# Identity and mask made on the chip, the first weight pieces fetched apart, and four steps moved in the order of a recurrent attention and feed-forward kernel

## The chip, the cores and the metric

The kernel runs on one core of a Trainium2 chip. The core has a matrix engine (TensorE, PE in the profile), a vector engine (VectorE, DVE), a scalar engine (ScalarE, ACT), a general one (GpSimd, POOL) and an engine that issues most of the transfers (SyncE, SP). Each runs its own instruction queue in order and waits for the others through semaphores. TensorE writes into PSUM, a small memory of eight banks that VectorE and ScalarE read; everything else lies in SBUF, 128 partitions wide.

The metric is the device time of one execution in microseconds (us). Before the change the median of 8 runs is 381.15 us, with 380.92 the lowest and 381.96 the highest.

## The reference

The first half is a gated linear attention, a recurrence over 768 tokens for 4 batches and 8 heads of width 48; the second is a feed-forward block with a softmax-weighted activation and a layer norm.

```python
# attention: q, k, v, alpha are (4, 8, 768, 48), float32
for t in range(S):
    state = alpha[:, :, t, :, None] * state + np.einsum('bhd,bhe->bhde', k[:, :, t], v[:, :, t])
    y[:, :, t] = np.einsum('bhd,bhde->bhe', q[:, :, t], state)

# feed-forward on x = y as (3072 tokens, 384); w_in (384, 1024), w_out (1024, 384)
h = x @ w_in
e = np.exp(h - np.max(h, axis=-1, keepdims=True))
solu = h * e / (np.sum(e, axis=-1, keepdims=True) + 1e-09)
mu = np.mean(solu, axis=-1, keepdims=True)
var = np.mean((solu - mu) ** 2, axis=-1, keepdims=True)
return ((solu - mu) / np.sqrt(var + 1e-06) * g_ln) @ w_out
```

The two weight matrices arrive as 64-bit floats and are turned into 32-bit ones on the chip.

## The kernel before

The 768 tokens are cut into six groups of 128. A group holds 128 tokens of each of the four batches, 512 in all, and passes two phases. In the attention phase the recurrence is replaced by products within the group: alpha, keys and queries are turned so that the head width lies on the partitions (32 partitions for each batch; the 48 of a head are split into a block of 32 and, two heads together, one of 32, twelve blocks in all). Running products of alpha (`scan_back`, `scan_on`, both the scan of L222) scale keys (L243) and queries (L254); TensorE forms scores (L281), which are masked to the lower triangle (L292) and multiplied with the values (L315) beside a product with the state carried from earlier groups; `next_state` (L364, L374) carries the state on. In the up phase the 1024 hidden columns are taken in eight tiles f of 128: `up_mm` (L389) multiplies, `up_act` forms the exponential on ScalarE (L403), the product h times e on VectorE (L404) and its square on ScalarE (L405); `running` (L420) adds up squares on VectorE and exponentials on GpSimd. `down` (L500) multiplies by the second weights, chunk by chunk of 128 tokens; `finish` (to L541) forms the norm from the sums (L523, L525, L528 on VectorE, L537 on GpSimd), for the first group adds the mean's part (L533), scales on ScalarE (L539) and writes out.

All order is written out by hand; nothing is scheduled automatically. Four PSUM banks `a0` to `a3` serve attention, two `h` the up phase, two `o` the down phase.

**The start.** SP issues the first loads in this order: alpha, k, q, v (two transfers each, rows of 48 floats), and the first four of eight weight pieces with `fetch` (L569). ACT's queue loads the 128x128 identity, the mask (ones on and above the diagonal), a parity table and the gains. GpSimd clears buffers: `vt`, `unit`, `aT`, `hT`, `seed`, `state`. VectorE sets constants, `ones` first among them. TensorE then runs 16 matmuls on `ones` alone to warm up and turns alpha, k and q by matmuls with the identity (L171).

`fetch(i, slot, n)` brings n pieces beginning with piece i into the slots of 1536 floats of `room` that begin at `slot`. A piece of w_in is 256 of its columns in 64 bits, over three blocks of 128 rows; `fetch(0, 3, 2)` brings pieces 0 and 1 with three transfers of 512 KB whose rows hold both. `bits(i, part)` turns a piece into 32-bit floats in five VectorE operations: part 0 is L599 and L602, part 1 is L607, L610 and L611; without a part both are done. `in_range(i)` tests a piece's size on ScalarE (L586, L587).

**The first group.** After the scores of both halves of the heads, VectorE masks batches 0 and 1 of the first half (`masked(0, range(2))`), while ScalarE copies batches 2 and 3 out and GpSimd masks them (L712, L713). VectorE then masks all four batches of the second half (`masked(1)`) and converts piece 0 (`bits(0)`). `read_values(0)` on TensorE takes batch after batch; each needs heads of both halves. Behind it on TensorE stand the turning of the gains and of the keys (`keys_back`, L300, copied out by ScalarE in L302) and the first up tile, which needs piece 0 converted.

**The turn to the second up phase.** While group 0's output and group 1's attention end, group 2's alpha and keys are prepared: three backward scans, the turning of the keys (L197, L200), their product on GpSimd (L243, two operations), and `scan_on(2, 2)`, the forward scan of the third block of four. Then come `read_values(1)`, a test of alpha on ScalarE (L214) and the last part of chunk 3's `down`, with `finish(3)` at the end. The loop over up phases g = 1 to 5 follows; in step s of eight it runs up tile s, then what the plan names under `behind`: for g = 1 in step 0 the state and the v load, in step 1 the forward scans of blocks 0 and 1 (`on0 on1`), in step 2 the turning of the queries' last 16 (`lasts`, L200, followed by GpSimd's product with `qe`) and of their first 32 (`firsts`, L197, followed by two products with `qv`), in step 3 `apart` (L247). `running` comes after `behind`; `after` names the chunk whose `finish` runs behind the next up tile.

Of the kernel before, what the change touches and what calls it, by code (L numbers as in the profile page):

```python
# [14 lines left out]
ALU = mybir.AluOpType  # L15
AX = mybir.AxisListType
P = 128
# [15 lines left out]
def fast_path(ctx, tc, q, k, v, alpha, moe_w_in, moe_w_out, moe_g_ln, out):  # L33
# [12 lines left out]
    nc = tc.nc  # L46
    B, H, S, D = q.shape
# [30 lines left out]
    ident = const.tile([P, P], FP, name="ident")  # L78
    mask = const.tile([P, P], FP, name="mask")
    ones = const.tile([P, P], FP, name="ones")  # L80
# [148 lines left out]
    def scan_on(g, i):  # L229
        part = slice(NP * i, NP * i + NP)  # L230
        if i == 2:

            nc.vector.reciprocal(out=seed[:, :, 0:1], in_=h4[:, :, 1:2])
            nc.scalar.copy(out=fend[:, g], in_=h4[:, :, 1])
        scan(aT[:, part], aT[:, part], seed[:, part], False)
# [53 lines left out]
    def masked(half, batches=range(B)):  # L289
        a = masks[half]  # L290
        for b in batches:
            nc.vector.tensor_tensor(  # L292
                out=sT[:, b, half * NP : half * NP + NP], in0=a[b], in1=mask[:, None, :].to_broadcast([P, NP, P]),
                op=ALU.mult,
            )
# [47 lines left out]
    def read_values(g, batches=range(B)):  # L343
        if 0 in batches:
            gr[g]["x"] = pair.tile([P, KC, B, P], FP, name="x")
        for b in batches:
            for n, part in enumerate(parts):
                for a, r, h, e in part:
                    y_mm(b, a, r, 0, vn[:, b, h, e], sT[:, b, h], n == len(parts) - 1)
        for b in batches:  # L350
            nc.scalar.copy(out=gr[g]["x"][:, :, b], in_=reading["y"][b])
# [159 lines left out]
    def finish(n):  # L511
        g, b = divmod(n, B)
        d = st[n]
        s, o = sums[:, n], d["o"][:, 0:DM]
        t0 = b * S + g * P
        if g == G - 1:
            o_sb = work.tile([P, DM], FP, name="o_sb")
            r = gr[g]["r"][:, b : b + 1]
            nc.scalar.activation(out=o_sb, in_=o, func=AF.Copy, scale=r)
            nc.scalar.dma_start(out=out[t0 : t0 + P, :], in_=o_sb)  # L520
            d.clear()
            return
        nc.vector.tensor_copy(out=s[:, 0:1], in_=d["o"][:, DM : DM + 1])  # L523
        t = small.tile([P, 1], FP, name="t")
        nc.vector.scalar_tensor_tensor(  # L525
            out=t, in0=s[:, 0:1], scalar=-1.0 / DFF, in1=s[:, 0:1], op0=ALU.mult, op1=ALU.mult
        )
        nc.vector.tensor_tensor(out=s[:, 3:4], in0=t, in1=gr[g]["s"][:, b : b + 1], op=ALU.add)  # L528
        if g == 0:

            if not d.get("moved"):
                o = work.tile([P, DM + 1], FP, name="o_mean")[:, 0:DM]
            nc.vector.scalar_tensor_tensor(  # L533
                out=o, in0=mean_sb, scalar=s[:, 0:1], in1=d["o"][:, 0:DM], op0=ALU.mult, op1=ALU.add
            )
        r = small.tile([P, 1], FP, name="r")
        nc.gpsimd.tensor_tensor(out=r, in0=s[:, 3:4], in1=mhalf, op=ALU.pow)  # L537
        o_sb = work.tile([P, DM], FP, name="o_sb")
        nc.scalar.activation(out=o_sb, in_=o, func=AF.Copy, scale=r)  # L539
        nc.sync.dma_start(out=out[t0 : t0 + P, :], in_=o_sb)  # L540
        d.clear()  # L541
# [16 lines left out]
    def fetch(i, slot, n=1):  # L558

        kind, f = pieces[i]  # L560
        w = n * F // (2 if kind else KC)
        raw = room[:, 1536 * slot : 1536 * (slot + n)].bitcast(U32).rearrange("p (c f w) -> p c f w", f=w, w=2)
        if kind:
            parts = [(slice(0, P), c, moe_w_out[(f + c) * P : (f + c + 1) * P, :]) for c in range(2)]
        else:
            parts = [(slice(0, P), c, moe_w_in[c * P : (c + 1) * P, f * P : f * P + w]) for c in range(KC)]
        for rows, c, src in parts:
            if float64:
                nc.sync.dma_start(out=raw[rows, c].rearrange("p f w -> p (f w)"), in_=src.bitcast(U32))  # L569
            else:  # L570
                dst = w_out[rows, f + c, 0:DM] if kind else w_in[rows, c, f * P : f * P + w]
                nc.sync.dma_start(out=dst, in_=src)
        for m in range(n):
            raws[i + m] = raw[:, :, w // n * m : w // n * (m + 1)]
# [14 lines left out]
    def bits(i, part=None):  # L589
        if not float64:  # L590
            return
        lo, hi = raws[i][:, :, :, 0], raws[i][:, :, :, 1]
        if part != 1:
            made[i] = [
                two.tile([P, F], FP, tag="two", name=x).rearrange("p (c f) -> p c f", c=hi.shape[1])
                for x in ("top", "low")
            ]
            top = made[i][0].bitcast(U32)
            nc.vector.tensor_scalar(  # L599
                out=top, in0=hi, scalar1=3, scalar2=0x3FFFFFF8, op0=ALU.logical_shift_left, op1=ALU.bitwise_and  # L600
            )
            nc.vector.scalar_tensor_tensor(  # L602
                out=top, in0=hi, scalar=0xC0000000, in1=top, op0=ALU.bitwise_and, op1=ALU.bitwise_or
            )
        if part != 0:
            top, low = made.pop(i)
            nc.vector.tensor_scalar(  # L607
                out=low.bitcast(U32), in0=top.bitcast(U32), scalar1=0xFF800000, scalar2=None, op0=ALU.bitwise_and
            )
            nc.vector.scalar_tensor_tensor(out=low, in0=lo, scalar=2.0**-52, in1=low, op0=ALU.mult, op1=ALU.mult)  # L610
            nc.vector.tensor_tensor(out=place(i), in0=low, in1=top, op=ALU.add)  # L611
# [34 lines left out]
    def inline(x, name):  # L646
        return nc.inline_tensor(np.ascontiguousarray(x, np.float32), name=name).ap()

    load_first(alpha, an, 0)
    nc.scalar.dma_start(out=ident, in_=inline(np.eye(P), "ident_c"))  # L650
    nc.scalar.dma_start(out=mask, in_=inline(np.triu(np.ones((P, P))), "mask_c"))
    odd = np.arange(P) // E1 % 2
    nc.scalar.dma_start(out=parity, in_=inline(np.stack([1 - odd, odd], 1), "parity_c"))
    nc.scalar.dma_start(out=g_rows, in_=moe_g_ln.rearrange("(c p) -> c p", p=P))
# [7 lines left out]
    nc.gpsimd.memset(seed, 0.0)  # L662
    nc.gpsimd.memset(state, 0.0)
    load_v_first(0)
    fetch(0, 3, 2)
    fetch(2, 1, 2)
    nc.vector.memset(ones, 1.0)
    nc.vector.memset(small_ones, 1.0 / 32)
    nc.vector.memset(mhalf, -0.5)
    nc.vector.memset(mone, -1.0)  # L670
# [26 lines left out]
    for i in (2, 0, 1):  # L697
        if i == 1:
# [3 lines left out]
            out=qe if i == 2 else qv[:, part], in0=t[i], in1=aT[:, part, 1:SW], op=ALU.mult  # L702
# [7 lines left out]
    for b in (2, 3):  # L710
        s = sT[:, b, 0:NP]
        nc.scalar.copy(out=s, in_=masks[0][b])  # L712
        nc.gpsimd.tensor_tensor(out=s, in0=s, in1=mask[:, None, :].to_broadcast([P, NP, P]), op=ALU.mult)  # L713
    masked(0, range(2))
    masked(1)
    bits(0)
    read_values(0)
    gains()
    keys_back(0)
# [94 lines left out]
    for i in range(3):  # L814
# [2 lines left out]
    keys(2)  # L817
    load(k, kn, 3)
    scan_on(2, 2)
    read_values(1)  # L820
    alpha_over(2)
    load(alpha, an, 3)
    down(3, 1, slice(3, HF))
    finish(3)

# [2 lines left out]
        behind={0: "states v keys", 1: "load on2 on0 on1", 2: "lasts firsts", 3: "apart", 5: "decay", 6: "alpha", 7: "back"},  # L830
# [2 lines left out]
    )  # L833
    first = dict(
        head={3: "keys_back", 5: "masked0", 6: "masked1"},
        behind={0: "states v", 1: "on0 on1", 2: "lasts firsts", 3: "apart", 5: "decay", 7: "alpha back"},
        tail={4: "scores0", 5: "scores1", 6: "begin read0 read1"},
        middle={7: "read2 read3 values"},
    )
# [51 lines left out]
    for g in range(1, G + 1):  # L891
        rise, att = g < G, g + 1 < G
        plan = first if g == 1 else usual

        def at(where, s):
            for what in plan[where].get(s, "").split() if att else ():
                attend(g + 1, what)

        after = None
        if not rise:  # L900
            break
        for s in range(FC):
            at("head", s)
            if rise:
                up(g, s)
            if after is not None:
                finish(after)
                after = None
            if s == 0 and g > 1:
                token_sums(g - 1)  # L910
            at("behind", s)
            for f in centres.get(s, ()) if g == 1 else ():
                centre(f)
            if rise and s:
                running(g, s)
            at("middle", s)
            if rise and s == FC - 1:
                todo.append((g * B, 0))
            step = todo.pop(0)
            if step:  # L920
                n, half = step
                down(n, half)
                if half:
                    after = n
            at("tail", s)
        if after is not None:
            finish(after)
        todo = [(n, half) for n in range(g * B, g * B + B) for half in range(2)][1:]
# [492 lines left out]
```

## Time and profile before

| what | us |
| --- | --- |
| median of 8 runs | 381.15 |
| the profiled execution | 380.4 |
| its span | 378.6 |
| TensorE busy, of the span | 365.6 (97%) |
| VectorE busy | 244.1 (64%) |
| ScalarE busy | 146.9 (39%) |
| GpSimd busy | 128.4 (34%) |
| TensorE's granted clock, mean | 0.997 |

The span runs from the first instruction to the end of the last one; the rest of the profiled execution's time lies around it. A matmul's end is modelled, so TensorE's busy share says little of how much it could still take. In a timeline row the first number is the start in us, the second the length of the row, then engine, line of the kernel, operation, what is written and read (partitions x elements), how many equal instructions the row joins, and in brackets how long the engine was idle before and what ended that. "issue" names a wait that the profile can't put down to anything.

### The profile page before, as it was taken

Reading aid. Unit: us, or ns where it says so; the run is one execution under the profiler, and the core shown is the slowest. Engines: PE = TensorE matmul, PEld = TensorE weight load, DVE = VectorE, ACT = ScalarE, POOL = GpSimd, SP = SyncE. Lnnn points to the kernel's source line nnn. Section 1 sums busy time; section 2 is a strip of 40 time slices with the busy share of each in tenths; the row PEclk is TensorE's granted clock in tenths of the full one; section 3 lists DMA queues with packets and bytes.
Section 4 is the critical chain, followed back from the end, with each engine's and each line's share of the span. In section 5 each row is a group of like instructions: output and inputs, shape, how many; then the busy total and the mean of one; then the engine's idle time right before and its main releaser. Section 6 shows DMA issues by size and latency. Waiting matters only on the chain.

```text
span 378.6 us, 10523 instructions
## 1 busy us (share of the span) xinstructions
PE 365.6 (97%) x4659; PEld 219.4 (58%) x4659; DVE 244.1 (64%) x379; ACT 146.9 (39%) x263; POOL 128.4 (34%) x134
## 2 busy tenths in 40 slices
PE   8789999999898999999999999999999999999995
PEld 8675355566654565555675555675556675555552
DVE  1988889979988876874665875665865411455410
ACT  3638874593445152224451224451233131233110
POOL 5040000042246970662630671630672420333210
PEclk9999999999999999999999999999999999999998
DMA  9984999304096001950002940002300000000011
GB/s 187 193 307 119 222 273 141 85 2 126 26 226 128 4 5 34 197 126 21 23 25 41 205 111 23 23 24 46 61 0 23 24 23 2 22 21 21 23 46 48
DMA packets 65526, 30.78 MB, mean 81 GB/s; under 512 B 47032, under 2 KB 63680, under 8 KB 65472
## 3 DMA queue, kind: packets, MB, share of 16 engines
q1 hardware_dynamic: 64448, 29.10, 34.5%
q10 hardware_dynamic: 1024, 0.92, 0.7%
q8 instruction: 38, 0.62, 0.7%
q14 instruction: 16, 0.13, 0.1%
HBM read 25.30 MB, written 4.72 MB: 79 GB/s over the span
## 4 chain that ended last, share of the span: by engine, by line
PE 72%; DVE 14%; ACT 5%; issue 3%; DMA 3%; SPq 2%; POOL 0%; ACTq 0%; DVEq 0%
PE o L500 30%; PE h L389 24%; PE y L315 8%; PE a L281 5%; SPq L153 2%; DVE hT L222 2%; DVE room L404 2%; DMA qn<-in_q_dram 2%; DVE sT L292 1%; ACT sq L586 1%; DMA out_dram<-o_sb 1%; DVE aT L197 1%; PE kv L364 1%; PE tp L300 1%; DVE top L602 1%
## 5 line engine op out<-in xcount | busy, mean ns | idle before, releaser
L500 PE MATMUL o<-w_out,room 128*128 128x385 f32 x384 | 133.8, 491 | 0.0
L389 PE MATMUL h<-x,w_in 128*128 128x512 f32 x288 | 132.5, 599 | 0.6 <-DVE room L404 0.3
L500 PEld LDWEIGHTS o<-w_out,room 128*128 128x128 f32 x384 | 71.2, 190 | 55.8 <-issue 13.1
L389 PEld LDWEIGHTS h<-x,w_in 128*128 128x128 f32 x288 | 52.8, 189 | 59.8 <-issue 47.9
L404 DVE TENSOR_TENSOR room<-h,e 128x512 f32<-128x512 f32 x40 | 27.6, 689 | 82.0 <-ACT e L403 81.9
L403 ACT ACTIVATE e<-h 128x512 f32<-128x512 f32 x40 | 23.9, 598 | 107.5 <-PE h L389 107.5
L420 POOL TENSOR_TENSOR p<-p,e 128x512 f32<-128x512 f32 x30 | 41.8, 1394 | 15.7 <-ACT e L403 15.6
L537 POOL TENSOR_TENSOR r<-sums,mhalf 128x1 f32<-128x1 f32 x20 | 14.9, 745 | 78.6 <-DVE sums L528 78.5
L405 ACT ACTIVATE u<-room 128x512 f32<-128x512 f32 x40 | 25.2, 631 | 36.9 <-DVE room L404 36.9
L292 DVE TENSOR_TENSOR sT<-a,mask 128x512 f32<-128x512 f32 x42 | 26.1, 682 | 8.3 <-PE a L281 8.2
L263 POOL TENSOR_TENSOR state<-state,hT 128x192 f32<-128x192 f32 x20 | 11.2, 580 | 52.8 <-DVE hT L222 52.8
L243 POOL TENSOR_TENSOR kT<-kT,hT 128x1024 f32<-128x1024 f32 (+1 forms) x8 | 14.2, 1798 | 42.2 <-DVE kT L197 42.2
L222 DVE TENSOR_TENSOR_SCAN hT<-aT,unit 128x516 f32<-128x516 f32 x18 | 23.1, 1347 | 7.6 <-ACT aT L683 7.5
L420 DVE TENSOR_TENSOR p<-p,u 128x512 f32<-128x512 f32 x30 | 23.0, 768 | 6.5 <-ACT u L405 6.5
L281 PEld LDWEIGHTS a<-qv,kT 32*128 32x128 f32 x704 | 21.9, 186 | 8.7 <-issue 2.4
L281 PE MATMUL a<-qv,kT 32*128 32x128 f32 x704 | 24.7, 278 | 1.9 <-POOL qv L254 1.1
L222 DVE TENSOR_TENSOR_SCAN aT<-aT,seed 128x516 f32<-128x516 f32 x18 | 26.3, 1494 | 0.2
L315 PE MATMUL y<-sT,vn 128*32 128x128 f32 x768 | 23.6, 274 | 2.2 <-issue 1.7
L315 PEld LDWEIGHTS y<-sT,vn 128*32 128x32 f32 x768 | 20.9, 110 | 4.4 <-issue 3.4
L214 ACT ACTIVATE sq<-an,mone 128x1536 uint8<-128x1536 f32 x12 | 18.9, 1574 | 0.2
L315 PE MATMUL y<-qv,state 32*32 32x128 f32 x960 | 16.6, 277 | 0.0
L539 ACT ACTIVATE o_sb<-o,r 128x384 f32<-128x384 f32 x16 | 9.3, 581 | 18.8 <-POOL r L537 18.8
(146 smaller groups left out, 371.9 us busy)
## 6 DMA issues: line engine op xcount, KB each, us to landing
an<-in_alpha_dram SPq DMA_DIRECT2D x20, 192.0 KB, 4.5
vn<-in_v_dram SPq DMA_DIRECT2D x10, 384.0 KB, 6.3
out_dram<-o_sb SPq DMA_DIRECT2D x20, 192.0 KB, 1.9
room<-in_moe_w_in_dram SPq DMA_DIRECT2D x6, 512.0 KB, 8.1
room<-in_moe_w_out_dram SPq DMA_DIRECT2D x8, 384.0 KB, 4.3
kn<-in_k_dram SPq DMA_DIRECT2D x16, 192.0 KB, 4.5
qn<-in_q_dram SPq DMA_DIRECT2D x16, 192.0 KB, 3.7
kn<-in_k_dram SPq DMA_DIRECT2D x4, 384.0 KB, 5.8
```

Of the source, the lines that this page charges most:

```text
L214: nc.scalar.activation(out=sq, in_=x, func=AF.Relu, scale=sign, bias=mone, accum_out=over[:, g, i : i + 1])
L222: nc.vector.tensor_tensor_scan(out=o, data0=a, data1=s, initial=1.0, op0=ALU.mult, op1=ALU.add)
L281: nc.tensor.matmul(a[b][:, i], lhsT=kT[quarter(b), kb], rhs=qv[quarter(b), qb], start=kb == h, stop=kb != h, tile_position=(32 * b, 0), sk ...
L292: nc.vector.tensor_tensor(out=sT[:, b, half * NP : half * NP + NP], in0=a[b], in1=mask[:, None, :].to_broadcast([P, NP, P]), op=ALU.mult,)
L315: nc.tensor.matmul(y_bank(b)[quarter(r), a], lhsT=lhsT, rhs=rhs, start=(b, r) not in begun, stop=stop, tile_position=(row, 32 * r), skip_g ...
L389: nc.tensor.matmul(h, lhsT=w_in[:, a, f * P : (f + 1) * P], rhs=d["x"][:, a].rearrange("p b t -> p (b t)"), start=(a == 0), stop=(a == KC ...
L403: nc.scalar.activation(out=e, in_=h, func=AF.Exp)
L404: nc.vector.tensor_tensor(out=u, in0=h, in1=e, op=ALU.mult)
L405: nc.scalar.activation(out=u2, in_=u, func=AF.Square)
L420: eng.tensor_tensor(out=p, in0=d[0][i] if f == 1 else p, in1=d[f][i], op=ALU.add)
L500: nc.tensor.matmul(d["o"][:, 0 : DM + 1], lhsT=u_of(g, f)[:, b * P : b * P + P], rhs=w_out[:, f], start=(f == 0), stop=(f == FC - 1), skip ...
L537: nc.gpsimd.tensor_tensor(out=r, in0=s[:, 3:4], in1=mhalf, op=ALU.pow)
```

## The change

- The loads of the identity and the mask on ACT's queue go. VectorE's setting of `ones` moves up, and GpSimd makes both matrices from it with two `affine_select` operations at the head of its queue, before it clears buffers.
- Pieces 0 and 1 are fetched by two calls instead of one: six transfers of 256 KB instead of three of 512 KB, and each piece lies in a slot of its own, with its 768 numbers of 64 bits in one run.
- Part 0 of `bits(0)` stands between `masked(0, range(2))` and `masked(1)`, part 1 behind `masked(1)`.
- `finish(3)` moves from before the loop to step 0 of g = 1, behind the first up tile and ahead of the state.
- The forward scan of block 0 of group 2 moves from step 1 to before `read_values(1)`, directly behind that of block 2.
- `lasts` moves from step 2 to step 1, ahead of the forward scan of block 1.

```diff
     load_first(alpha, an, 0)
-    nc.scalar.dma_start(out=ident, in_=inline(np.eye(P), "ident_c"))
-    nc.scalar.dma_start(out=mask, in_=inline(np.triu(np.ones((P, P))), "mask_c"))
+    nc.vector.memset(ones, 1.0)
+    for x, op in ((ident, ALU.is_equal), (mask, ALU.is_ge)):
+        nc.gpsimd.affine_select(
+            out=x, in_=ones, pattern=[[1, P]], compare_op=op, fill=0.0, base=0, channel_multiplier=-1
+        )
...
     load_v_first(0)
-    fetch(0, 3, 2)
+    fetch(0, 3)
+    fetch(1, 4)
     fetch(2, 1, 2)
-    nc.vector.memset(ones, 1.0)
...
     masked(0, range(2))
+    bits(0, 0)
     masked(1)
-    bits(0)
+    bits(0, 1)
     read_values(0)
...
     scan_on(2, 2)
+    scan_on(2, 0)
     read_values(1)
     alpha_over(2)
     load(alpha, an, 3)
     down(3, 1, slice(3, HF))
-    finish(3)
...
     first = dict(
...
-        behind={0: "states v", 1: "on0 on1", 2: "lasts firsts", 3: "apart", 5: "decay", 7: "alpha back"},
+        behind={0: "states v", 1: "lasts on1", 2: "firsts", 3: "apart", 5: "decay", 7: "alpha back"},
...
-        after = None
+        after = B - 1 if g == 1 else None
```

## The prediction

> **What bounds the kernel now.** I read the page's busy shares and its chain first, then the chain in order of time, then the timelines of the two stretches that the change touches.
>
> ```profile
> PE   8789999999898999999999999999999999999995
> PE 72%; DVE 14%; ACT 5%; issue 3%; DMA 3%; SPq 2%; POOL 0%; ACTq 0%; DVEq 0%
> ```
>
> From about 129 us on, the chain is PE alone without a hole, so time won or lost there can't be made up: whatever shift exists at 129 us reaches the end. Before that the chain changes hands, and these pieces of it say who sets the first up phase:
>
> ```profile
> 24.55 3.04 PE y L315 x101
> ...
> 28.36 0.90 ACT kg L302 x2
> ...
> 29.92 0.90 ACT sq L586 x2
> ...
> 31.82 1.04 ACT sq L586 x2
> ...
> 33.81 0.49 ACT sT L403
> ```
>
> The y matmuls of read_values end at 27.59; then ScalarE works without a gap (kg copies, two range tests) up to the first exponential. ScalarE, not DVE, holds the pace until 56.49 us; DVE waits before almost every L404. So this stretch is as late as y's end, and DVE work finished earlier gains nothing in it. From 57 to 105 us DVE runs back to back.
>
> The stretch of the masks:
>
> ```profile
> 20.18 1.29 DVE L292 TENSOR_TENSOR sT<-a,mask 128x512 f32<-128x512 f32 x2 [0.30 <-PE a L281]
> 22.01 1.29 DVE L292 TENSOR_TENSOR sT<-a_h,mask 128x512 f32<-128x512 f32 x2 [0.55 <-PE a_o L281]
> 24.82 0.95 DVE L599 TENSOR_SCALAR top<-room 128x768 uint32<-128x768 uint32 x1 [0.32 <-DMA room<-in_moe_w_in_dram]
> 25.80 0.96 DVE L602 SCALAR_TENSOR_TENSOR top<-room,top 128x768 uint32<-128x768 uint32 x1
> ...
> 48.34 0.55 DVE L599 TENSOR_SCALAR top<-room 128x768 uint32<-128x768 uint32 x1
> ```
>
> ```profile
> 20.93 2.51 POOL L713 TENSOR_TENSOR sT<-sT,mask 128x512 f32<-128x512 f32 x2 [0.20 <-ACT sT L712]
> ```
>
> ```profile
> 22.75 1.07 PE L315 MATMUL y<-sT,vn 128*32 128x128 f32 x23 [0.42 <-DVE sT L292]
> 24.55 3.04 PE L315 MATMUL y<-sT,vn 128*32 128x128 f32 x101 [0.72 <-issue]
> ```
>
> DVE idles 0.55 + 0.32 = 0.87 us around the masks. PE resumes y at 22.75, when the first mask of the second half is done (22.01 + 0.69), and has one hole of 0.72.
>
> The turn of the stages, DVE and GpSimd:
>
> ```profile
> 103.04 2.40 DVE L222 TENSOR_TENSOR_SCAN aT<-aT,seed 128x516 f32<-128x516 f32 x1
> 105.52 0.91 DVE L525 SCALAR_TENSOR_TENSOR t<-sums 128x1 f32<-128x1 f32 x1
> 108.42 0.69 DVE L404 TENSOR_TENSOR room<-h,e 128x512 f32<-128x512 f32 x1 [1.27 <-ACT e L403]
> 110.90 2.96 DVE L222 TENSOR_TENSOR_SCAN aT<-aT,seed 128x516 f32<-128x516 f32 x2
> 115.94 2.05 DVE L197 STREAM_TRANSPOSE qv<-qn 128x1024 f32<-128x1024 f32 x1
> ```
>
> ```profile
> 102.17 4.24 POOL L243 TENSOR_TENSOR kT<-kT,hT 128x1024 f32<-128x1024 f32 x2 [8.29 <-DVE kT L197]
> 110.33 1.30 POOL L420 TENSOR_TENSOR p<-e 128x512 f32<-128x512 f32 x1 [3.08 <-ACT e L403]
> 116.22 1.18 POOL L254 TENSOR_TENSOR qe<-qe,aT 128x512 f32<-128x512 f32 x1 [4.59 <-DVE qe L200]
> ```
>
> The reader is to see how one engine holds up the other. A scan takes 1.2 us (two in 2.4), but 2.40 beside the key product; a 128x1 operation usually of 0.16 takes 0.91 and ends with the key product (102.17 + 4.24 = 106.41). Each waits until the GpSimd product that runs is over, and a GpSimd product that comes meanwhile waits in turn. Transposes (one input) are not held: 2.05 beside qe. L292 and L404, with one input in PSUM, aren't either.
>
> **The start.** Two loads of 64 KB leave ACT's queue. By bytes, 131 KB at the page's 187 to 193 GB/s is 0.69 us; by rows, alpha, k and q are 12,288 rows landing in about 12.7 us, so 256 rows are 0.26, part of them sent before alpha. I take 0.2 us (0 to 0.69): alpha's scan at 8.61 and q's transposes at 14.66 both move, so masked(0) ends at 21.27 instead of 21.47. The two GpSimd selections have no row. Bounds: a quarter of the 0.53 memset (0.1) to a whole 512 product (1.3) each. PE's warming covers the identity until 6.46; `unit`, ready at 3.17, becomes ready by 6.1 at worst and is read after 8.4; so they cost nothing unless the pair takes over 4.9 us. Moving `ones` up moves nothing behind it.
> [...]
>
> **The fetch.** Three issues become six, each about 0.44 us on SP; pieces 2 and 3, then 1.3 us later in issue, land near 28.5 and are read at 35, which covers that. Piece 0 is half of the 1.57 MB that landed at 24.8; at 307 GB/s (page, third slice) it lands 2.6 us earlier, near 22.0 after the 0.2; at the earliest soon after v, whose copy starts at 19.13. An early landing changes nothing, since DVE asks for it at 21.24. Fetched alone its rows are contiguous, as piece 4's are, so L599 falls from 0.95 to 0.55 (those are its bounds).
>
> **Half a conversion between the masks.** L599 wants to start at 21.24, inside the first GpSimd mask (20.73 to 22.0 after the shift; the second to 23.24). Is it held? It has one input, like the transposes, but at 768 words in 0.55 us it reads 1.4 words/ns, like the two-input p<-u,u (1024 in 0.66: 1.55), not like a transpose (1024 in 2.05: 0.5). I count it as held: 22.0 to 22.47. Then the second GpSimd mask, waiting, runs to 23.65, and L602, with two inputs, waits for it and ends at 24.5. A landing after 22.0 puts L599 behind the second mask instead and ends at 24.7. masked(1) is queued behind L602, and PE's y waits for it: first mask done at 24.45 + 0.69 = 25.14, against 22.70. PE then needs 28 + 96 = 124 records at 27.6 ns (2.76/100) plus 0.28: y ends at 25.19 + 3.42 + 0.28 = 28.9 instead of 27.6, since 0.72 of hole goes away. **+1.3 us**, the start's gain included. Other ends: L599 at 0.95 and not held, L602 behind the second mask, done at 24.1: +0.9. L599 at 0.55 and not held, L602 asking at 21.8, before the second mask: -0.3; with 0.69 at the start, -0.8. Hole not gone: +2.0. The half conversion left over ends at 29.5, before PE has finished the key transposes at 30.5: hidden.
> [...]
>
> **The turn.** finish(3) goes behind the first L404, scan_on(2,0) in front, the qe transpose (1.1 us) before scan_on(2,1). GpSimd's queue now has qe's product ahead of its first p. ScalarE is free at 105.0, so the exponential e ends at 105.6 and the 1.27 us hole goes. Then: first scan done 105.44; the second is held by the key product to 106.43, done 107.55; L404 to 108.2; finish 108.1 to 109.15 (now unheld); state sums to 110.2. But o_sb (L539, 0.62) stands before the next exponential on ScalarE, r on GpSimd (0.55) before it: that exponential ends at 110.4, against 110.26, so the second L404 gains nothing: 111.1. qe's transpose to 112.1; scan_on(2,1) 112.0 to 113.2; qe's product, held, 113.2 to 114.35; p<-u,u behind it to 114.95 (this wait of 1.15 is new); third L404 114.9 to 115.6, against 115.04. Only one transpose is left after it, but ScalarE sets the fourth: square 116.2, three kg copies (1.54) 117.7, exponential 118.2, L404 at 118.25 against 118.45. apart, scores and masks follow: **-0.2 us**. Unheld, the third L404 would come at 113.8 and the fourth at 117.4 (ScalarE) or earlier: -1.1. A late r: +0.3. SP's order of the out write and the v load stays; v, issued at 108.72, goes 2 us later and is read at 137.
>
> **Sum.** +1.3 - 0.2 = +1.1 us on a profiled execution of 380.4 (span 378.6 and 1.8 around it), so 381.5 there; the median of 8 runs stands 0.75 above it at 381.15: **382.2 us**. A measurement here tells 0.2%, 0.76 us, from no change.
>
> **Rivals.**
> - Two-way cancelling: L599 isn't held and stays near +0.9, and the turn gives 0.2 to 1.1. +0.9 - 0.6 = +0.3: 381.4, no change. For it: one input; the hole of 1.27 is real. Against: two holds are shown at the turn's places. 30%.
> - [...] 14%.
> - [...] 6%.
>
> The forecast has 50%, and 381.6 to 382.9 of its own. Range 380.6 to 383.1: up to y's hole staying (+0.7), down through the cancelling case with the turn at its best. Faster 0.14, same 0.31, slower 0.55.
>
> **What would show it.** Right: L602 between the masks at over 1.5 us, PE's y ending near 28.9, the first exponential (L403) near 35.0; no 1.27 hole at the turn, but a p<-u,u of about 1.8 there; the scores (L281) of the second up phase begin within 0.5 us of 119.6 plus the shift. Wrong: L602 at 0.96 in place, y ending by 27.6, or the fourth L404 over 0.8 us earlier against y's end.

## The result and the profile after

| | before | changed |
| --- | --- | --- |
| median | 381.24 us (31 runs) | 382.76 us (11 runs) |
| lowest to highest | 380.55 to 382.64 | 382.06 to 383.32 |
| profiled execution, its span | 380.4, 378.6 | 383.03, 381.3 |
| ratio of the runs, 95% interval | | 1.0036 (1.0026 to 1.0047) |

The changed kernel is slower by about 1.4 us. The page of the changed kernel, with the rows that answer to those of before (40 slices of 9.5 us; then the chain that ended last):

```profile
PE   8869999999998999999999999999999999999995
...
PEclk9989999999999999999999999999999999999999
...
PE 70%; DVE 12%; ACT 7%; SPq 4%; issue 3%; DMA 2%; ACTq 0%; DVEq 0%
```

From the fourth slice on nothing has changed in kind. What is new stands in the third slice (19 to 28.6 us): TensorE is busy for 6 tenths of it instead of 8, and its granted clock is 8 tenths. The rows of VectorE, GpSimd and TensorE there, from the timeline (start, length, engine, line, operation):

```profile
20.52 1.29 DVE L292 TENSOR_TENSOR sT<-a,mask 128x512 f32<-128x512 f32 x2 [0.30 <-PE a L281]
22.23 0.73 DVE L599 TENSOR_SCALAR top<-room 128x768 uint32<-128x768 uint32 x1 [0.42 <-DMA room<-in_moe_w_in_dram]
22.99 1.90 DVE L602 SCALAR_TENSOR_TENSOR top<-room,top 128x768 uint32<-128x768 uint32 x1
24.82 1.28 DVE L292 TENSOR_TENSOR sT<-a_h,mask 128x512 f32<-128x512 f32 x2
...
31.27 0.56 DVE L599 TENSOR_SCALAR top<-room 128x768 uint32<-128x768 uint32 x1
```

```profile
21.27 2.81 POOL L716 TENSOR_TENSOR sT<-sT,mask 128x512 f32<-128x512 f32 x2 [0.47 <-ACT sT L715]
```

```profile
22.27 0.41 PE L315 MATMUL y<-sT,vn 128*32 128x128 f32 x4
25.55 5.35 PE L315 MATMUL y<-sT,vn 128*32 128x128 f32 x124 [2.87 <-DVE sT L292]
```

L602, 0.96 us elsewhere, takes 1.90: it ends 0.81 us, nearly its own time, after the GpSimd masks (L713 before, L716 now; 21.27 + 2.81 = 24.08). So masked(1) begins at 24.82 instead of 22.01, and TensorE has a hole of 2.87 us. That much was forecast. The y matmuls behind the hole were not: 124 records take 5.35 us, where the rate of before would give 3.7. The windows view says why (stretch, length, busy time and number of each engine, granted clock, share of the DMA engines, GB/s):

```profile
22.00:24.00 2.00, 0.68 (x17) 0.29 (x12) 1.74 (x2) 0.00 (x0) 2.00 (x2) 1.00 0.89 197
24.00:26.00 2.00, 0.45 (x16) 0.45 (x18) 2.00 (x3) 0.00 (x0) 0.14 (x2) 1.00 0.99 331
26.60:30.00 3.40, 3.40 (x76) 3.27 (x67) 3.07 (x5) 0.97 (x3) 0.00 (x0) 0.50 0.52 211
30.00:32.00 2.00, 2.00 (x38) 1.78 (x31) 0.86 (x3) 1.27 (x3) 0.00 (x0) 0.99 0.00 0
```

In the last column but two stands TensorE's clock: 1.00, then 0.50 for the 3.4 us from 26.6 to 30.0, then full again. Half speed for 3.41 us (26.63 to 30.04 in the trace) costs 1.7 us of matmul time. The first exponential of the up phase, before and in the changed kernel:

```profile
33.72 0.58 ACT L403 ACTIVATE sT<-h 128x512 f32<-128x512 f32 x1
```

```profile
37.05 0.58 ACT L403 ACTIVATE sT<-h 128x512 f32<-128x512 f32 x1
```

It comes 3.33 later, and nearly all of the lateness is carried to the turn (3.22 at 94 us, 3.1 to 3.2 at 103).

The turn gives back 0.8 of it (2.38 from 126 us on). Its rows on VectorE and GpSimd:

```profile
108.47 2.15 DVE L222 TENSOR_TENSOR_SCAN aT<-aT,seed 128x516 f32<-128x516 f32 x1
110.54 0.66 DVE L404 TENSOR_TENSOR room<-h,e 128x512 f32<-128x512 f32 x1
...
113.45 0.69 DVE L404 TENSOR_TENSOR room<-h,e 128x512 f32<-128x512 f32 x1 [0.21 <-ACT e L403]
...
116.12 1.61 DVE L420 TENSOR_TENSOR p<-u,u 128x512 f32<-128x512 f32 x1
117.65 0.68 DVE L404 TENSOR_TENSOR room<-h,e 128x512 f32<-128x512 f32 x1
...
120.97 0.69 DVE L404 TENSOR_TENSOR room<-h,e 128x512 f32<-128x512 f32 x1
```

```profile
115.36 1.81 POOL L254 TENSOR_TENSOR qe<-qe,aT 128x512 f32<-128x512 f32 x1 [3.08 <-ACT e L403]
```

Taking the 3.22 of 94 us off these starts, the four L404 stand at 107.32, 110.23, 114.43 and 117.75, against 108.42, 110.29, 114.36 and 118.45 before: the first gains 1.10, the second and third nothing, the fourth 0.70.

### The profile page after: what moved, and what is told of

The parts are those of the page before. It is cut to its first block, busy times and chain, and to the rows that moved or that the text cites. A ratio compares the mean times of both kernels' runs of the same rounds, so it can differ in the third digit from the quotient of the medians.

```text
span 381.3 us, 10529 instructions
## 1 busy us (share of the span) xinstructions
PE 367.2 (96%) x4659; PEld 221.7 (58%) x4659; DVE 244.3 (64%) x379; ACT 146.4 (38%) x263; POOL 130.4 (34%) x136
## 4 chain that ended last, share of the span: by engine, by line
PE 70%; DVE 12%; ACT 7%; SPq 4%; issue 3%; DMA 2%; ACTq 0%; DVEq 0%
PE o L500 30%; PE h L389 24%; PE y L315 9%; PE a L281 5%; SPq L153 2%; DVE hT L222 2%; DVE room L404 2%; DVE top L602 2%; DVE sT L292 1%; DMA an<-in_alpha_dram 1%; ACT sq L586 1%; DMA room<-in_moe_w_in_dram 1%; SPq L189 1%; DVE aT L197 1%; PE kv L364 1%
## 5 line engine op out<-in xcount | busy, mean ns | idle before, releaser
L404 DVE TENSOR_TENSOR room<-h,e 128x512 f32<-128x512 f32 x40 | 27.6, 690 | 81.4 <-ACT e L403 81.4
L315 PE MATMUL y<-sT,vn 128*32 128x128 f32 x768 | 24.8, 286 | 3.7 <-DVE sT L292 2.9
L222 DVE TENSOR_TENSOR_SCAN aT<-aT,seed 128x516 f32<-128x516 f32 x18 | 26.6, 1510 | 0.2
L315 PEld LDWEIGHTS y<-sT,vn 128*32 128x32 f32 x768 | 22.3, 115 | 5.8 <-DVE sT L292 3.1
```

The source lines that it names most:

```text
L222: nc.vector.tensor_tensor_scan(out=o, data0=a, data1=s, initial=1.0, op0=ALU.mult, op1=ALU.add)
L315: nc.tensor.matmul(y_bank(b)[quarter(r), a], lhsT=lhsT, rhs=rhs, start=(b, r) not in begun, stop=stop, tile_position=(row, 32 * r), skip_g ...
L404: nc.vector.tensor_tensor(out=u, in0=h, in1=e, op=ALU.mult)
```

## The experiments

Three theories stood at the outset. A: the half conversion between the masks is the loss, by its hold and by the drop of the clock behind the hole. B: the loss is the start, where the first scan begins at 9.10 instead of 8.61. C: the half conversion costs the forecast's 1.3 alone, and the rest lies elsewhere. Each result is the ratio to the kernel before, run beside it on the same chip, with its 95% interval in brackets.

A number used below is the mean granted clock of an execution, which is known for every execution, not only the profiled one. One stretch of 3.41 us at half clock takes 3.41 / 2 / 381 = 0.0045 off it; the last microseconds, behind the last matmul, take off 0.003 in the profile of before (half clock for 2.16 us, from 376.44 to the end). So 0.997 to 1.0 is read as an execution without such a stretch, 0.996 and less as one with it. By this measure 12 of the 13 recorded executions of the changed kernel, the profiled one among them, had such a stretch; the thirteenth (0.998) is the fastest of them, 382.06.

**e1_no_half, e12_no_half_again: the change without the half conversion.**

```diff
     masked(0, range(2))
-    bits(0, 0)
     masked(1)
-    bits(0, 1)
+    bits(0)
```

> The changed kernel with the whole conversion of piece 0 behind masked(1) again; everything else as changed. Theory A (the half conversion between the masks is the loss: L602 held to 24.89 behind GpSimd's masks, masked(1) 2.8 us later, and then a hole of 2.87 us in TensorE after which its granted clock is 0.5 for 3.41 us): masked(1) starts near 22.35, no stretch at clock 0.5 after 6 us, y ends near 27.9, the first exponential near 34.1; the median falls by 2.4 to 3.0, to 379.8 to 380.4, below both kernels. Theory B (the loss is the later start, the first scan at 9.10 instead of 8.61, because GpSimd makes identity and mask): the median stays above 382.2. Theory C (the half conversion costs only the 1.3 forecast, the rest is elsewhere): 381.3 to 381.6.

> The version without the half conversion once more, as the neighbour of the last one on the same chip: ratio 0.993 to 0.9965, mean clock 0.997 or more in every execution.

Measured: 379.43 us, ratio 0.9948 (0.993 to 0.9965), and again 379.37, 0.9953 (0.9934 to 0.9972); mean clock 0.998 to 1.0 in all 18 executions. From the first one's profile, VectorE and TensorE:

```profile
21.74 1.29 DVE L292 TENSOR_TENSOR sT<-a_h,mask 128x512 f32<-128x512 f32 x2 [0.55 <-PE a_o L281]
...
24.14 0.55 DVE L599 TENSOR_SCALAR top<-room 128x768 uint32<-128x768 uint32 x1
24.73 0.96 DVE L602 SCALAR_TENSOR_TENSOR top<-room,top 128x768 uint32<-128x768 uint32 x1
```

```profile
22.48 1.07 PE L315 MATMUL y<-sT,vn 128*32 128x128 f32 x23 [0.42 <-DVE sT L292]
24.26 3.04 PE L315 MATMUL y<-sT,vn 128*32 128x128 f32 x101 [0.71 <-issue]
```

masked(1) stands at its old place, L602 is 0.96, and y ends at 27.3. The one moved half conversion is worth 1.0036 - 0.9950 = 0.0086, 3.3 us: more than the whole loss, and a little over theory A's 2.4 to 3.0, within the interval. Without it the other edits beat both kernels. Theory B falls, and so does C: 1.3 is too little.

**e2_half_only: the kernel before with the separate fetch and the half conversion.**

```diff
-    fetch(0, 3, 2)
+    fetch(0, 3)
+    fetch(1, 4)
...
     masked(0, range(2))
+    bits(0, 0)
     masked(1)
-    bits(0)
+    bits(0, 1)
```

> The kernel before with the separate fetch and the half conversion between the masks alone. Theory A: all of the loss and more, 2.4 to 3.0 above before, 383.6 to 384.2, since the turn's gain is missing; L602 near 1.9, a hole of over 2.4 in TensorE before y. Theory B: no loss, 381.2. Theory C: 1.3 above, 382.5.

Measured: 384.41, ratio 1.0059 (1.0038 to 1.008), 2.2 us, a little under theory A's 2.4 to 3.0 and within the interval; five of the six executions have a mean clock of 0.995 or less. The loss is there without the other edits, and with another order of the holds:

```profile
22.54 1.50 DVE L599 TENSOR_SCALAR top<-room 128x768 uint32<-128x768 uint32 x1 [0.95 <-DMA room<-in_moe_w_in_dram]
24.07 0.96 DVE L602 SCALAR_TENSOR_TENSOR top<-room,top 128x768 uint32<-128x768 uint32 x1
```

Here the piece landed while a GpSimd mask ran, so L599 waited (1.50 instead of 0.55) and L602 did not. The pair takes the same time from its start to its end: 2.49 here, 2.66 in the changed kernel. The hole was 3.23 us, and the clock dropped twice (mean 0.989): behind the hole, where y's 124 records took 5.35 us again, and at the turn, which is unchanged from before in this kernel:

```profile
121.00:125.20 4.20, 2.68 (x50) 1.58 (x52) 3.23 (x5) 2.40 (x5) 3.59 (x3) 1.00 0.64 149
125.20:128.60 3.40, 3.40 (x31) 2.14 (x24) 2.71 (x4) 0.63 (x1) 3.32 (x4) 0.50 0.25 52
128.60:132.00 3.40, 3.40 (x64) 2.13 (x67) 2.21 (x4) 0.82 (x2) 3.30 (x5) 1.00 0.00 0
```

**e7_dve_masks: no GpSimd in that stretch.**

```diff
-    for b in (2, 3):
-        s = sT[:, b, 0:NP]
-        nc.scalar.copy(out=s, in_=masks[0][b])
-        nc.gpsimd.tensor_tensor(out=s, in0=s, in1=mask[:, None, :].to_broadcast([P, NP, P]), op=ALU.mult)
-    masked(0, range(2))
+    masked(0)
     bits(0, 0)
```

> The changed kernel with all four batches of the first half masked on VectorE (no copies on ScalarE, no products on GpSimd there). If GpSimd's masks hold L602 (1.90 instead of 0.96): L599 starts near 23.0 with 0.55, L602 is 0.96, masked(1) begins near 24.5 although two more masks of 0.6 stand before it; as the hole in TensorE stays (22.3 to 25.2) so does the drop of its clock, and the median is 0 to 0.4 below the changed kernel's 1.0036 of before: 1.0025 to 1.0036. If L602 is long for another reason (its transfer, its place behind the masks): it is still near 1.9, masked(1) begins near 25.5, and the ratio is 1.006.

Measured: 381.9, ratio 1.0004 (0.9989 to 1.0019), below the expected band. The profile's rows:

```profile
20.20 2.48 DVE L292 TENSOR_TENSOR sT<-a,mask 128x512 f32<-128x512 f32 x4 [0.30 <-PE a L281]
22.60 0.55 DVE L599 TENSOR_SCALAR top<-room 128x768 uint32<-128x768 uint32 x1
23.18 0.96 DVE L602 SCALAR_TENSOR_TENSOR top<-room,top 128x768 uint32<-128x768 uint32 x1
24.06 1.28 DVE L292 TENSOR_TENSOR sT<-a_h,mask 128x512 f32<-128x512 f32 x2
```

```profile
24.80 5.35 PE L315 MATMUL y<-sT,vn 128*32 128x128 f32 x124 [2.44 <-DVE sT L292]
```

Without GpSimd both operations have their own length, so the hold is GpSimd's. VectorE does two more masks and masked(1) still comes sooner (24.06 against 24.82): the two masks given to GpSimd here cost more than they save. The hole, now 2.44 us, cost the clock in only half of the executions: of twelve, six have a mean clock of 0.999 (median 381.5) and six 0.995 or 0.996 (median 382.3). The expectation had the drop in all of them; that was the miss.

**e4_bridge and e8_bridge24: the hole filled with matmuls that nobody needs.**

```diff
     scores(0, 1, t)
+    warm(26, ps_a, "a3")
     read_begin()
```

> The changed kernel with 26 matmuls on ones (0.112 us each, 2.9 us) queued on TensorE in front of the first y, so that the hole of 2.87 us before 25.55 is filled; VectorE and GpSimd are left alone. If the clock dropped to 0.5 because of the hole, and in most executions: no stretch at 0.5 there, y ends near 29.2 instead of 30.9, median 1.0 to 1.7 lower, 381.1 to 381.8. If the drop is a rare accident of the profiled execution: 382.8 still, with the profile's y at 29.2. If y is slow for another reason (weights, transfers): y still ends near 30.9 and the clock drops all the same.

Each such matmul is two records, so this put 52 of them (6.07 us) in front of y and held y up itself: 383.56, ratio 1.0052 (1.0038 to 1.0065). It still showed y's 128 records taking 3.70 us at full clock, and a mean clock of 0.997 to 0.999 in all its executions. With `warm(12, ps_a, "a3")` instead:

> The first bridge put twice the records meant on TensorE (52, 6.07 us) and so held y up itself. Now 12 matmuls on ones, 24 records, 2.8 us, in front of y. If the drop to 0.5 follows from the hole: no stretch at 0.5, y starts near 25.3 and ends near 29.0 (3.70 for its 128 records at full clock, as the first bridge showed) instead of 30.9; the median falls by 1.2 to 1.7 against the changed kernel, to a ratio of 0.9992 to 1.0005. If the changed kernel is slow for the hold alone and the drop is rare: ratio 1.003 or more.

Measured: 381.83, ratio 1.001 (0.9996 to 1.0024); mean clock 0.997 to 1.0 in all eleven executions. TensorE in its profile:

```profile
21.64 2.94 PE L445 MATMUL warm<-ones 128*128 128x128 f32 x24
24.52 0.41 PE L315 MATMUL y<-sT,vn 128*32 128x128 f32 x4
25.26 3.69 PE L315 MATMUL y<-sT,vn 128*32 128x128 f32 x124 [0.33 <-DVE sT L292]
```

With TensorE kept busy the same y takes 3.69 us instead of 5.35. VectorE and GpSimd have the same work (masked(1) begins at 24.52), so the drop follows from the hole. Against the changed kernel the ratio falls by 0.0026, 1.0 us, less than the trace's 1.66 but within the two intervals. What is left against e1 is the hold alone: 1.6 us at y's end (28.95 against 27.30), 1.9 at the first exponential (35.41 against 33.49) and 0.0060, 2.3 us, by the ratios.

**e9_late_half: the half conversion two masks later.**

```diff
     masked(0, range(2))
-    bits(0, 0)
-    masked(1)
+    masked(1, range(2))
+    bits(0, 0)
+    masked(1, range(2, 4))
     bits(0, 1)
```

> The changed kernel with the half conversion two masks later, between batches 1 and 2 of masked(1). Then GpSimd's masks are over (23.5) and TensorE has the y of two batches to do. If hold and hole are the loss: L599 0.55 and L602 0.96 unheld, masked(1) begins at 22.3, hole in TensorE under 1.5, no drop in most executions, y ends near 28.2; ratio 0.995 to 0.997, near the version without the half conversion (0.9948). If any half conversion between the masks costs its own 1.6 us: y ends near 29.2 and the ratio is 0.999.

Measured: 380.12, ratio 0.9964 (0.9949 to 0.998), mean clock 0.999 to 1.0. VectorE in its profile:

```profile
23.28 0.69 DVE L599 TENSOR_SCALAR top<-room 128x768 uint32<-128x768 uint32 x1
24.00 0.96 DVE L602 SCALAR_TENSOR_TENSOR top<-room,top 128x768 uint32<-128x768 uint32 x1
```

L599 met the end of a GpSimd mask, L602 has its own length, and y ended at 27.56, 0.26 later than in e1. By the ratios this is 0.5 us worse than e1 and e12, within the noise. So half a conversion among the masks cost little here (0.26 us at y's end), where GpSimd had finished (its masks end at 23.50) and TensorE had other batches to work on. It gained nothing either: ScalarE, not VectorE, held the pace behind it, without a gap from 28.34 to the exponential at 33.75.

**e3_turn_only: the kernel before with the three moves at the turn.**

```diff
     scan_on(2, 2)
+    scan_on(2, 0)
     read_values(1)
...
     down(3, 1, slice(3, HF))
-    finish(3)
...
-        behind={0: "states v", 1: "on0 on1", 2: "lasts firsts", 3: "apart", 5: "decay", 7: "alpha back"},
+        behind={0: "states v", 1: "lasts on1", 2: "firsts", 3: "apart", 5: "decay", 7: "alpha back"},
...
-        after = None
+        after = B - 1 if g == 1 else None
```

> The kernel before with finish, scan and lasts moved at the turn alone. If the 0.8 us that the changed kernel won back between 103 and 126 us is the turn's own: 380.4. If it is the forecast's 0.2: 381.0. If it was only slack that the lateness ran into (the same places wait anyway when everything comes 3 us earlier): 381.2. In the first case the scores of the second up phase begin 0.8 earlier than 119.6, in the last within 0.1 of it.

Measured: 380.39, ratio 0.997 (0.9956 to 0.9983), 1.1 us. The first scores of the second up phase, before and here:

```profile
119.61 0.50 PE L281 MATMUL a<-qv,kT 32*128 32x128 f32 x8 [1.14 <-POOL qv L254]
```

```profile
119.00 0.50 PE L281 MATMUL a<-qv,kT 32*128 32x128 f32 x8 [0.77 <-POOL qv L254]
```

They come 0.6 earlier although this execution came to the turn 0.16 late, so the trace shows 0.8 of the gain, the first of the three cases. The rest fits the clock. All twelve of its executions have a mean clock of 0.997 or more; of the 73 executions of before in these comparisons 38 have, with medians of 381.0 to 381.2 by chip, and nearly all the others have 0.993 or less, with medians of 381.9 to 382.1. The profiled execution of before was one of the first kind.

**e10_turn_filler: the hole at the turn filled instead.**

```diff
         elif what[:6] == "scores":
+            if what == "scores0" and a == 2:
+                warm(5, ps_a, "a3")
             scores(a, int(what[6]))
```

> The kernel before with 5 matmuls on ones (10 records, 1.12 us) on TensorE ahead of the scores of the second up phase, in the hole of 1.14 us at 118.47. If a part of the executions of before loses its clock for 3.41 us behind that hole (their mean clock is 0.993 or less, and 0.997 to 1.0 in the others; the half conversion alone showed such a stretch at 125.2 to 128.6), and this is what the moves at the turn also take away: the mean clock is at least 0.996 in every execution, and the ratio is 0.997 to 0.999. If the low mean clock has another place: about four in ten executions still have 0.993 or less, ratio 0.9995 to 1.0005.

Measured: 380.73, ratio 0.9987 (0.9975 to 0.9999); the mean clock is 0.997 to 1.0 in all twelve executions, while 15 of the 26 of before beside it have 0.993 or less. TensorE in its profile:

```profile
118.75 1.28 PE L445 MATMUL warm<-ones 128*128 128x128 f32 x10
120.06 0.51 PE L281 MATMUL a<-qv,kT 32*128 32x128 f32 x8
```

Nothing but ten records of useless work was added. So the kernel before loses its clock behind this hole in about half of its executions (35 of the 73 have a mean of 0.996 or less), and the moves at the turn take that away too.

**e11_no_lasts: `lasts` left where it was.** On e1:

```diff
-        behind={0: "states v", 1: "lasts on1", 2: "firsts", 3: "apart", 5: "decay", 7: "alpha back"},
+        behind={0: "states v", 1: "on1", 2: "lasts firsts", 3: "apart", 5: "decay", 7: "alpha back"},
```

> The version without the half conversion (ratio 0.9948), with lasts left in step 2 as before; finish and the scan of block 0 stay moved. If the gain at the turn comes from the third and fourth L404 (the fourth only as early as ScalarE's three copies allow) and the hold of p<-u,u behind qe's product (1.61 instead of 0.66) is a loss: p<-u,u 0.66, the third L404 1 us earlier, the fourth 0 to 0.4 earlier, ratio 0 to 0.001 lower than its neighbour's. If moving lasts ahead is what gains: the fourth L404 waits behind 3.2 us of transposes and comes 0.3 or more later, ratio 0.001 higher.

Measured: 379.38, ratio 0.9945 (0.9927 to 0.9963), not to be told from the 0.9953 of its neighbour e12, run beside it. VectorE in its profile:

```profile
112.30 0.66 DVE L420 TENSOR_TENSOR p<-u,u 128x512 f32<-128x512 f32 x1
112.88 0.68 DVE L404 TENSOR_TENSOR room<-h,e 128x512 f32<-128x512 f32 x1
...
117.00 0.67 DVE L404 TENSOR_TENSOR room<-h,e 128x512 f32<-128x512 f32 x1
```

The hold of p<-u,u is gone, and against its neighbour, at whose turn everything stands 0.23 earlier, the third L404 is 1.2 and the fourth 0.4 earlier; at 128 us 0.2 of that is left. So finish and the scan together carry the gain at the turn; moving `lasts` adds nothing that can be measured.

**e5_ident_only: the kernel before with identity and mask made on GpSimd.** The edit is the first hunk of the change, with the old setting of `ones` taken out.

> The kernel before with identity and mask made on GpSimd alone. Theory A (the later first scan in the changed kernel's profile, 9.10 against 8.61, is only the place where TensorE's clock rises, 6.15 instead of 4.39, which differs from execution to execution): alpha lands 0.3 earlier; with the rise near 4.4 the first scan is 0.25 and the first mask 0.17 earlier than before, with a rise near 6 it is later; median 0.2 below before (ratio 0.9985 to 1.0000). Theory B (GpSimd's two selections hold the start up): first scan 0.5 later wherever the clock rises, ratio 1.0009 or more.

Measured: 381.71, ratio 1.0009 (0.9994 to 1.0024). That is the lower edge of theory B's band and above theory A's, but the interval reaches into both, so the median can't tell them apart. Among the executions that kept their clock (0.997 or more) the medians are 381.25 with the edit and 381.2 without. The traces say more. TensorE's warming at the start, in the profiles of the changed kernel, e1, e5 and e12 in this order:

```profile
1.10 6.23 PE L445 MATMUL warm<-ones 128*128 128x128 f32 x32 [1.10 <-DVE w_out L674]
```

```profile
1.11 5.39 PE L445 MATMUL warm<-ones 128*128 128x128 f32 x32 [1.11 <-DVE w_out L674]
```

```profile
1.11 6.77 PE L445 MATMUL warm<-ones 128*128 128x128 f32 x32 [1.11 <-DVE w_out L673]
```

```profile
1.11 5.18 PE L445 MATMUL warm<-ones 128*128 128x128 f32 x32 [1.11 <-DVE w_out L674]
```

The same 32 records take 5.18 to 6.77 us, because the rate of TensorE rises from half to full at a different moment in each execution: their spacing goes from 0.213 to 0.112 us at 3.95 to 7.29 us in the thirteen profiles of this study (at 4.39 in before, at 6.15 in the changed kernel). When the rise comes late, warming is still running as alpha lands, and the first scan waits: in the changed kernel alpha has landed at 6.52 and warming ends at 7.33, in before 6.83 and 6.46. Among executions with the rise between 4.29 and 4.40 the first scan begins at 8.52 and 8.61 with the loads (e3 and before) and at 8.25 and 8.27 with GpSimd's matrices (e4 and e1). With the rise at 6.15 it is 9.10 (the changed kernel), at 7.29 it is 9.65 (e5). With the rise at 5.74 to 5.93 the two kinds no longer differ: 8.88 and 8.97 with the loads (e2, e10), 8.93 with GpSimd's matrices (e11). So theory A stands in the traces: the edit gains about 0.3 at the first scan where the rise is early and nothing where it is late, and the later start of the changed kernel's profile is the moment of the rise.

## Why the prediction came out as it did

The time lies 0.6 us from the forecast, and the sign is right. But two of its terms were off, in opposite directions, and their errors cancel in part, and that the sum came out so near is luck: on the scale of the profile 381.5 was forecast and 383.03 measured, 1.5 off, and the 0.75 added for the median made up most of it, though the changed kernel has no such distance (its median of 382.76 lies under the 383.03 of its profile).

- **The bound.** A shift at 129 us reaches the end: 2.38 there, 2.7 at the end of the span; the other 0.3 comes at 142 us, where TensorE waits 0.46 inside y and waited 0.15 before, so the chain was not quite without a hole. VectorE does not run back to back from 57 to 105 us either: from 77 to 90 it is busy for 10.4 of 13.0 us. The lateness passed through all the same.
- **The start.** -0.2 was forecast. At the first mask e1, with nearly the same rise of the clock as e3, is 0.17 earlier; with a late rise nothing is left, and the median does not resolve it. The selections take 0.29 each, near the lower bound, at 1.13 us, where VectorE's last constant ends, so without a delay.
- **The fetch.** Piece 0 landed at 22.11 (forecast 22.0). L599 alone is 0.55, as taken.
- **The half conversion: the hold.** Right in kind, and closely sized. From the end of masked(0) to the end of L602 the forecast had 3.23 us; the trace has 3.08. The way there was another: L599 waited for its piece, not for a mask, and fell between the two masks (0.73), so L602 alone was held for long. A landing after 22.0 was to put L599 behind the second mask; e2 shows that case. That L599 would be held was an estimate from its rate, with the transposes' row (2.05 beside qe) against it; its 1.50 there shows it. By e8 against e1 the hold is worth 1.6 us at y's end and 1.9 at the first exponential; the forecast's +1.3, which had the start's 0.2 in it, makes it 1.5.
- **The half conversion: y.** This is the step that failed: "PE then needs 28 + 96 = 124 records at 27.6 ns (2.76/100) plus 0.28". At full clock that is exact, 3.70 against 3.69 in e8. But the step carried the rate of a TensorE that had never been idle for long over to one that had just stood still for 2.87 us. In the trace it took 5.35. y ended at 30.9 instead of 28.9, and the first exponential came at 37.05 instead of 35.0. Of these 2.0 us 1.65 is the clock; most of the rest is that masked(0) ended at 21.81 and not 21.27, in an execution whose clock rose late at the start.
- **The turn.** The mechanism was right: the hole of 1.27 goes, the second L404 gains nothing, p<-u,u is held (1.61; forecast 1.8), ScalarE sets the fourth L404. The fourth was mis-sized: "L404 at 118.25 against 118.45", a gain of 0.2; it came at 117.75 on the same scale, a gain of 0.7. The error lies ahead of the third L404, set at 114.9 and come at 114.43: the working set rows end to end that overlap by about 0.1 each (the second scan ends at 112.98, not 113.2) and gave the held product 1.15 after the scan where it took 0.97. From there to the fourth, the forecast's 2.6 us is what it took. Unseen was the rest of the gain: the hole there costs before its clock in about half of its executions (35 of 73). Together 1.1 us by e3, not 0.2.
- **The base.** "The median of 8 runs stands 0.75 above it" was taken as a constant of measuring. The profiled execution of before was one that kept its clock; the median lies among both kinds.
- **The rivals.** Cancelling did not happen. The faster outcome, given 0.14, needed L602 and p<-u,u both without a hold: in every profile with the half conversion beside GpSimd's masks either L602 waits (1.90 in the changed kernel, 1.91 in e4) or L599 (1.50 in e2, 1.68 in e8), and p<-u,u took 1.61.
- **The signs.** Three of those named came (L602 at 1.90, the 1.27 hole gone, p<-u,u at 1.61), three did not (y's end, the first exponential, and the scores, which begin at 121.98, 0.8 earlier than 119.6 plus the shift of 3.2). The fourth L404 stands 0.80 earlier against y's end, just where the forecast put its sign of being wrong.

Three runs on the kernel before hold the whole change between them: e2 (the fetch and the half conversion) +2.2 us, e3 (the turn) -1.1, e5 (identity and mask) +0.3. They add up to the measured 1.4, each with an interval of 0.5 to 0.8 us either way. In the changed kernel the half conversion is worth more, 3.3 (e1, e12). The separate fetch was not run alone; what it is worth by itself stays open.

## What to carry to other kernels

A wait in front of TensorE can cost more than its length: behind the hole of 2.87 us here the clock stood at 0.50 for 3.41 us, and y took 5.35 us instead of 3.69. Look at the granted clock just behind every hole (at the turn 1.20 us with 0.33 close behind went with a lost clock in e2, and by e10 so did 1.14 with 0.32 in about half of the executions of before), and price the work behind it at both rates. Before putting VectorE work into a gap, look at what GpSimd runs there: here an operation with two inputs (L602, 1.90 us instead of 0.96) and one with a single input (L599, 1.50 instead of 0.55) were both held; two masks later the same work cost little (L599 0.69, L602 0.96). And where one kernel's times spread by 2 us, compare the mean clock of the executions before taking the profiled one as the base of a sum.

## What the hardware showed that was not expected

- The moves of TensorE's clock lay on a grid. In the traces of before and of the changed kernel every full stretch between two of them is a multiple of 3.413 us: 3.413 at half clock; 20.48 (six of them), 351.57 (103) and 372.05 (109) at full. The grid's place differs in each execution (first rise at 3.95 to 7.29 us, a spread of 3.34, nearly one such step). So, it seems, the same hole cost the clock in some executions and not in others: six of twelve for e7's 2.44 us. Holes of 2.44 (e7), 2.87 (the changed kernel) and 3.23 us (e2) were followed by a stretch at half clock, and at the turn of e2 so were 1.20 and 0.33 us in one step of the grid, with matmuls between them. Before's profile, with 1.14 and 0.32 at that place, kept its clock. Counted step by step from the first rise in the traces of before and of the changed kernel, every step with 2.34 us or more without a matmul ended in a drop (2.34 at the changed kernel's hole, 2.36 at before's end), and none with 1.46 or less did. The ends of matmuls are modelled, and where between these numbers the clock drops was not shown.
- Of two VectorE instructions that met GpSimd's masks one waited, whichever came while a mask ran: L602 for the changed kernel's and e4's (1.90 and 1.91 instead of 0.96), L599 for e2's and e8's (1.50 and 1.68 instead of 0.55). The pair took 2.5 to 2.7 us either way. The mask waited too: the second one took 1.57 in the changed kernel instead of 1.28 in before.
